# Eight unused words behind each 128-column block of the weights that TensorE loads

## The chip, the core and the metric

The kernel runs on one NeuronCore of one Trainium2 chip. The metric is the device time of one execution in microseconds (us), taken on the chip; lower is better. The profile is one execution that the hardware profiler recorded.

## The reference

Attention pools 12480 tokens of 128 channels into 32 rows (each of the 32 `inducing` rows attends to all tokens), every token then attends to the 32 pooled rows, and two feed-forward layers with 2048 hidden units follow, the first with a leaky rectifier, the second with `h * sigmoid(1.702 h)`.

```
def mab(q, kv):
    s = scale * (q @ kv.transpose(0, 2, 1))
    s = s - s.max(-1, keepdims=True)
    a = np.exp(s)
    a /= a.sum(-1, keepdims=True) + 1e-09
    return a @ kv
h = mab(I, x)            # I: the 32 inducing rows
x = mab(x, h)            # 12480 x 128
h = x @ w_in             # 128 -> 2048
x = np.maximum(0.01 * h, h) @ w_out        # 2048 -> 128
h = x @ w2_in
out = (h * (1.0 / (1.0 + np.exp(-1.702 * h)))) @ w2_out
```

The weights come as float64, x and `inducing` as float32.

## The kernel before

**Tiling.** The tokens are cut into 25 tiles. Tiles 0 and 24 have 352 tokens, the 23 between them 512. A tile lies channels by tokens, `[128, 512]`, so that a product has the tile as its moving operand and a block of 128 x 128 weights as its stationary operand. The 2048 hidden units are 16 blocks of 128 (`NF`).

**Precision.** Each float32 operand is split into two float32r halves (hi and lo), and a product is done as three passes: hi by hi, lo by hi, hi by lo. Weights are converted from float64 bits on the chip (`convert_stages`, the last step `upper` writes hi on ScalarE and lo on GpSimd) and then stay in SBUF.

**The layers.** `steps` runs over layer, tile and block, 800 steps in all. In a step `ffn_in` (L704) makes 128 hidden units of a tile in PSUM. In the first layer this is one product with `hw` (L709; the pooled rows are already multiplied into the first weights), in the second three products with the two halves of `w2` (L713 to L715). ScalarE and VectorE apply the activation and split it into `ghi` and `glo` (L723, L724 in the first layer, L729 to L731 in the second). `ffn_out` (L734) adds the block's part to the output tile `acc`, three products with the two halves of `v1` or `v2` (L741 to L743), `LOOK` = 3 steps behind. So a step is 4 products in the first layer and 6 in the second, 4000 in all, and each is preceded by the load of its own stationary block (LDWEIGHTS). The order is written out by hand (`manual_schedule`); the side work (conversion, attention weights of the next tiles, the linear part of the leaky unit) is hung on steps by the tables at the top.

**Where the weights lie.** `w1`, `w2` and `hw` are rows of 2048 words (4 bytes each) in every partition, a block being 128 neighbouring words, that is 512 bytes. `v1` and `v2` hold for each block hi and lo side by side, again 128 words each. So the byte addresses of all blocks of a matrix leave the same remainder by 512. In the built program that is 416 for every block of `hw`, `w1`, `w2`, `v1` and `v2`. The moving tiles `ghi`, `glo` and `at` begin at addresses that leave 480, `x2h` and `x2l` at addresses that leave 96. `w1` is a moving operand only (L638, where the stationary operands `hTl` and `hTh` leave 416 too); `w2` is put in the space of `w1` once that has been read.

Of the kernel before, what the change touches and what calls it, by code (L numbers as in the profile page):

```python
# [10 lines left out]
F32 = mybir.dt.float32  # L11
# [8 lines left out]
LOOK = 3  # blocks of hidden units between both products  # L20
TC = 4  # chunks of tokens in a token tile
ENDS = 88  # tokens of a chunk in the first and the last tile, 128 in the others
B = 32  # side of VectorE's transposed blocks
# [5 lines left out]
# pieces of x that blocks of weights are loaded before, the iterations of their conversion  # L29
W_LOADS = [6, 8]  # L30
W_STEPS = [0, 0, 1, 2, 2, 3]
# where the work beside the first two tiles goes, by their steps
# [14 lines left out]
def kernel(  # L47
# [10 lines left out]
    """float32 products run as float32r passes over halves: hi is a value's upper 12  # L58
    significant bits, lo = value - hi the others, both exact in float32r."""
# [23 lines left out]
    # token p * chunks + j of a part of x is row p of chunk j  # L83
# [4 lines left out]
    # token tiles that are loaded together  # L88
# [14 lines left out]
    def keep_busy(count):  # L103
        """TensorE's clock halves when it waits for long: products of zeros meanwhile."""
        for _ in range(count):
            nc.tensor.matmul(
                idle_ps[:, :256], idle[:, :P], idle[:, :256], start=True, stop=True
            )

# [1 line left out]
    CW = 512  # L111
    LOW = bits_f32(896 << 20)  # the words of 2^-127 and of float32's largest 2^127 * f
    HIGH = bits_f32((1150 << 20) | 0xFFEFF)

    def convert_stages(src, hi, lo):
        """src: [P, CW] of float64 bits. Its magnitude clamped to float32's range, sign,
        exponent and 23 fraction bits make a float32: hi is its rounding, lo the rest."""
        raw = conv.tile([P, 2 * CW], U32, tag="raw", name="raw", bufs=5)
        d = raw.rearrange("p (n w) -> p n w", w=2)
        v = conv.tile([P, CW], U32, tag="v", name="v", bufs=3)  # L120
        vf = v.bitcast(F32)
        if len(hi.shape) == 3:
            vo = vf.rearrange("p (f d) -> p f d", d=hi.shape[2])
        else:
            vo = vf

        def load():
            dst = raw if len(src.shape) == 2 else raw.rearrange(
                "p (f d) -> p f d", d=src.shape[2]
            )  # L130
            nc.sync.dma_start(out=dst, in_=src)

        def magnitude():
            nc.scalar.activation(out=vf, in_=d.bitcast(F32)[:, :, 1], func=AF.Abs)  # L134

        def clamp():
            nc.gpsimd.tensor_scalar(vf, vf, LOW, HIGH, op0=ALU.max, op1=ALU.min)  # L137

        def shift():
            nc.vector.tensor_scalar(  # L140
                v, v, 3, 0x3FFFFFFF, op0=ALU.logical_shift_left, op1=ALU.bitwise_and
            )

        def top():
            nc.vector.scalar_tensor_tensor(  # L145
                v, d[:, :, 1], 0xC0000000, v, op0=ALU.bitwise_and, op1=ALU.bitwise_or
            )

        def bottom():
            nc.vector.scalar_tensor_tensor(  # L150
                v, d[:, :, 0], 29, v, op0=ALU.logical_shift_right, op1=ALU.bitwise_or
            )

        def upper():
            nc.scalar.activation(out=hi, in_=vo, func=AF.Copy)
            nc.gpsimd.tensor_tensor(out=lo, in0=vo, in1=hi.bitcast(F32), op=ALU.subtract)  # L156

        return load, magnitude, clamp, shift, top, bottom, upper

    def matrix_in(src, name, tag):  # L160
        """[model, hidden]: a column block of hidden units is a stationary operand."""
        hi, lo = (wts.tile([P, DFF], F32R, name=f"{name}{h}", tag=f"{tag}{h}") for h in "hl")
        parts = []
        for o in range(0, DFF, CW):
            c = slice(o, o + CW)
            parts.append((src[:, c].bitcast(U32), hi[:, c], lo[:, c]))
        return (hi, lo), parts

    def matrix_out(src, name):
        """[hidden, model] by blocks of hidden units, hi and lo of a block side by side."""  # L170
        w = wts.tile([P, NF, 2, C], F32R, name=name)
        parts = []
        for o in range(0, DFF, CW):
            f = slice(o // P, (o + CW) // P)
            s = src[o : o + CW, :].bitcast(U32).rearrange("(f p) d -> p f d", p=P)
            parts.append((s, w[:, f, 0, :], w[:, f, 1, :]))
        return w, parts

    w1, w1_parts = matrix_in(moe_w_in, "w1", "w")
    v1, v1_parts = matrix_out(moe_w_out, "v1")  # L180

# [37 lines left out]
    # ---- pooling attention: a split of the softmax per quadrant of partitions, merged at  # L219
    # the end; each has a running maximum over the pieces ----  # L220
# [13 lines left out]
    nm = xnp.tile([P, NP], F32, name="nm")  # -SCALE * running maximum  # L234
# [29 lines left out]
    def scores(i):  # L264
        """Quadrant q: chunks q * n to q * n + n - 1 of the piece."""
        n = pieces[i]
        k = ch[starts[i]]
        w = n * k
        ps = s_t[i] = ps_h.tile([P, 512], F32, tag="h", name="s_ps")
        for q in range(NQ):  # L270
            b, o = divmod(q * n, TC)
            nc.tensor.matmul(  # L272
                ps[q * m : (q + 1) * m, :w], iT,
                xT[starts[i] + b][:, o * k : o * k + w], start=True, stop=True,
            )
        nc.vector.tensor_reduce(out=mx[:, i : i + 1], in_=ps[:, :w], axis=AX.X, op=ALU.max)
        if i == 0:
            nc.vector.tensor_scalar_mul(nm[:, :1], mx[:, :1], -SCALE)
        else:
            nc.vector.scalar_tensor_tensor(  # L280
                out=nm[:, i : i + 1], in0=mx[:, i : i + 1], scalar=-SCALE,
                in1=nm[:, i - 1 : i], op0=ALU.mult, op1=ALU.min,
            )
# [65 lines left out]
    def merge_max():  # L349
        """The quadrants' maxima, each beside the others of its row."""  # L350
# [129 lines left out]
    at_t = {}  # L480

    def weights_tile():
        """Rows (hi, lo, hi, lo) of a tile's weights, for rows (hi, hi, lo, lo) of what they
        weigh: all four products in one contraction."""
        return main.tile([P, TOK], F32R, tag="at", name="at", bufs=3)

    def token_tile(t):
        """One tile, tokens on partitions."""
# [59 lines left out]
    hl = [None] * NG  # by group: hi and lo of the weights, pooled row x token  # L548

    def token_group(g):  # L550
        """Four tiles, a tile's pooled rows on a quadrant of partitions."""
# [5 lines left out]
        def s0():  # L557
            ps = ps_h.tile([P, 512], F32, tag="h", name="s2_ps")
            for q, t in enumerate(tiles):
                # a short tile's own columns again behind it  # L560
# [56 lines left out]
    def rows_upper(dst, src, scale):  # L617
        """(hi, hi, lo, lo) by quadrants of scale * src, which is the same in each."""
# [10 lines left out]
    hTh, hTl = halves(hTf, "hT")  # L629
    hw = wts.tile([P, DFF], F32R, name="hw")  # L630
# [3 lines left out]
    def pooled_block(b):  # L634
        ps = hw_ps[b] = ps_h.tile([P, 512], F32, tag="h", name="hw_ps")
        c = slice(b * 512, (b + 1) * 512)
        for j, (a, w) in enumerate(((hTl, w1[1]), (hTl, w1[0]), (hTh, w1[1]), (hTh, w1[0]))):
            nc.tensor.matmul(ps, a, w[:, c], start=(j == 0), stop=(j == 3))  # L638

    def pooled_upper(b):  # L640
        rows_upper(hw[:, b * 512 : (b + 1) * 512], hw_ps[b], 1.0)

    def pooled_lower(b):
        rows_lower(hw[:, b * 512 : (b + 1) * 512], hw_ps.pop(b), 1.0)

    # the leaky unit is LEAK * h + (1 - LEAK) * relu(h); its linear part needs both
    # weights' product with the pooled rows alone
# [3 lines left out]
    def linear_transposed(b):  # L651
# [3 lines left out]
        for k in range(4):  # L655
            f = 4 * b + k
            nc.tensor.transpose(
                ps[:, k * P : (k + 1) * P], hw[:, f * P : (f + 1) * P].bitcast(F32), ident
# [5 lines left out]
    def linear_product(b):  # L664
        for k in range(4):
            f = 4 * b + k
            nc.tensor.matmul(
                lin_st["ps"][:, : 2 * C], lin_st[b][:, k, :],
                v1[:, f].rearrange("p h c -> p (h c)"),
# [7 lines left out]
    def linear_end():  # L677
        # hi and lo rows and columns added, the sum in each quadrant
# [8 lines left out]
    # pair[(s, k), (s', k')] = (k == k') for s in (0, 2)  # L687
# [16 lines left out]
    def ffn_in(l, t, f):  # L704
        ps = ps_h.tile([P, 512], F32, tag="h", name="h_ps")
        o = ps[:, : tok[t]]
        cols = slice(f * P, (f + 1) * P)
        if l == 0:
            nc.tensor.matmul(o, hw[:, cols], at_t[t], start=True, stop=True)  # L709
        else:  # L710
            hi, lo = x2h_t[t]
            wh, wl = late["w2"]
            nc.tensor.matmul(o, wh[:, cols], hi, start=True, stop=False)  # L713
            nc.tensor.matmul(o, wl[:, cols], hi, start=False, stop=False)  # L714
            nc.tensor.matmul(o, wh[:, cols], lo, start=False, stop=True)  # L715
# [31 lines left out]
    def x2_slot(t):  # L747
        """One that is free by then: its x and its group's weights have been read."""
# [18 lines left out]
    # work beside the layers, by the step that it goes with  # L767
# [5 lines left out]
    # the first weights' blocks as the first two tiles get to them  # L773
# [52 lines left out]
    late_matrix(matrix_in, moe2_w_in, "w2", ["w"], 60)  # L826
# [58 lines left out]
```

## Time and profile before

| | |
|---|---|
| time, median of 3 runs | 976.13 us (975.91 to 976.14) |
| profiled execution, span from its first to its last instruction | 974.8 us |
| median less that span: what lies around it | 1.3 us |
| TensorE products busy / weight loads busy | 963.9 us (99%) / 783.3 us (80%) |
| VectorE busy | 644.5 us (66%) |
| ScalarE busy | 787.8 us (81%) |
| GpSimd busy | 67.2 us (7%) |

The profiled execution's own time is known as its span; the median of the runs is 1.3 us longer. Products are pipelined: a product of 512 columns has a record of some 0.39 us, and the next begins 0.23 us after it began. So the busy share of TensorE tells only that a product was always under way. What the kernel pays for a product is the distance from its start to the next start, called its **pitch** below. It is read from the start times of a timeline, or as a stretch divided by the count of products in it.

### The profile page before, as it was taken

To read this page: it belongs to the slowest core of one execution; us is meant where nothing else is said; L and a number is where in the kernel's file an instruction comes from. 1 tells how busy PE (TensorE), PEld (TensorE's weight loads), DVE (VectorE), ACT (ScalarE), POOL (GpSimd) and SP (SyncE) were. 2 spreads that over 40 slices of the span, in tenths; PEclk is the share of its full clock that TensorE was granted. 3 is DMA by queue.
4 is the path that set the end of the run, shared out by engine and by line. 5 is a ranking of instruction groups with operands and counts; after the bars stand their busy time and mean duration, and the time that the engine had idled before them with its cause. 6 is when DMAs were issued, how large, how long until landed. Compare 5 with 4: busy or idle time off the path is not lost.

```text
span 974.8 us, 13366 instructions
## 1 busy us (share of the span) xinstructions
PE 963.9 (99%) x4630; PEld 783.3 (80%) x4630; DVE 644.5 (66%) x1049; ACT 787.8 (81%) x1378; POOL 67.2 (7%) x53
## 2 busy tenths in 40 slices
PE   9989999999999999999999999999999999999998
PEld 6667787887878878898888888888888888888887
DVE  4898788978878778765555555555555555555554
ACT  6576677767766666679999999999999999999997
POOL 1360021202200000000000000000000000000000
PEclk9999999999999999999999999999999999999999
DMA  9302120031000100000000000000000000000000
GB/s 340 98 1 55 33 65 22 7 93 33 23 23 7 27 12 23 8 1 8 12 11 12 11 12 22 11 11 11 12 12 12 11 11 18 16 12 12 12 11 19
DMA packets 15434, 27.99 MB, mean 29 GB/s; under 512 B 2358, under 2 KB 6870, under 8 KB 15366
## 3 DMA queue, kind: packets, MB, share of 16 engines
q1 hardware_dynamic: 15366, 27.14, 8.8%
q8 instruction: 36, 0.59, 0.2%
q14 instruction: 32, 0.26, 0.1%
HBM read 14.79 MB, written 6.39 MB: 22 GB/s over the span
## 4 chain that ended last, share of the span: by engine, by line
PE 96%; DVE 3%; DMA 0%; ACT 0%; issue 0%; SPq 0%; DVEq 0%; ACTq 0%
PE acc L743 18%; PE acc L742 18%; PE acc L741 18%; PE h_ps L715 9%; PE h_ps L713 9%; PE h_ps L714 9%; PE h_ps L709 9%; PE xT_ps L255 1%; DVE glo L724 1%; PE s_ps L272 1%; PE s_ps L563 1%; PE pv_ps L321 1%; PE acc L745 1%; PE p_ps L302 1%; DMA xn<-in_x_dram 0%; DVE v L145 0%
## 5 line engine op out<-in xcount | busy, mean ns | idle before, releaser
L731 DVE TENSOR_TENSOR glo<-g,ghi 128x512 fp32r<-128x512 f32 (+1 forms) x400 | 271.7, 679 | 238.9 <-ACT ghi L730 226.9
L723 ACT ACTIVATE ghi<-h_ps 128x512 fp32r<-128x512 f32 (+1 forms) x400 | 233.1, 587 | 101.6 <-PE h_ps L709 97.1
L743 PE MATMUL acc<-glo,v 128*128 128x512 f32 (+1 forms) x800 | 310.6, 388 | 0.8 <-DVE glo L724 0.6
L742 PE MATMUL acc<-ghi,v 128*128 128x512 f32 (+1 forms) x800 | 309.1, 386 | 0.5 <-POOL v L156 0.5
L741 PE MATMUL acc<-ghi,v 128*128 128x512 f32 (+1 forms) x800 | 308.2, 385 | 0.0
L724 DVE SCALAR_TENSOR_TENSOR glo<-h_ps,ghi 128x512 fp32r<-128x512 f32 (+1 forms) x400 | 263.4, 674 | 65.1 <-ACT ghi L723 61.7
L729 ACT ACTIVATE g<-h_ps 128x512 f32<-128x512 f32 (+1 forms) x400 | 234.8, 587 | 36.2 <-PE h_ps L715 0.5
L730 ACT ACTIVATE ghi<-g 128x512 fp32r<-128x512 f32 (+1 forms) x400 | 248.2, 620 | 12.6
L742 PEld LDWEIGHTS acc<-ghi,v 128*128 128x128 f32 x800 | 150.3, 188 | 33.5 <-POOL v L156 0.8
L743 PEld LDWEIGHTS acc<-glo,v 128*128 128x128 f32 x800 | 150.3, 188 | 33.2 <-DVE glo L724 3.5
L741 PEld LDWEIGHTS acc<-ghi,v 128*128 128x128 f32 x800 | 150.3, 188 | 28.6
L715 PE MATMUL h_ps<-x2l,w2h 128*128 128x512 f32 (+1 forms) x400 | 156.8, 392 | 0.0
L709 PE MATMUL h_ps<-at,hw 128*128 128x512 f32 (+1 forms) x400 | 155.4, 389 | 0.3 <-ACT at L543 0.3
L713 PE MATMUL h_ps<-x2h,w2h 128*128 128x512 f32 (+1 forms) x400 | 154.7, 387 | 0.0
L714 PE MATMUL h_ps<-x2h,w2l 128*128 128x512 f32 (+1 forms) x400 | 153.1, 383 | 0.0
L709 PEld LDWEIGHTS h_ps<-at,hw 128*128 128x128 f32 x400 | 75.1, 188 | 20.1 <-issue 3.6
L714 PEld LDWEIGHTS h_ps<-x2h,w2l 128*128 128x128 f32 x400 | 75.1, 188 | 16.1
L715 PEld LDWEIGHTS h_ps<-x2l,w2h 128*128 128x128 f32 x400 | 75.1, 188 | 15.6
L713 PEld LDWEIGHTS h_ps<-x2h,w2h 128*128 128x128 f32 x400 | 75.1, 188 | 15.5
L137 POOL TENSOR_SCALAR v<-v 128x512 f32<-128x512 f32 x16 | 31.7, 1983 | 59.3 <-ACT v L134 59.3
L759 ACT ACTIVATE x<-acc 128x512 f32<-128x512 f32 (+1 forms) x25 | 14.7, 587 | 7.7 <-PE acc L745 7.7
L762 DVE TENSOR_SCALAR o_t<-acc 128x512 f32<-128x512 f32 (+1 forms) x25 | 16.8, 671 | 0.5 <-PE acc L743 0.5
(117 smaller groups left out, 347.2 us busy)
## 6 DMA issues: line engine op xcount, KB each, us to landing
out_dram<-o_t SPq DMA_DIRECT2D x23, 256.0 KB, 2.0
xn<-in_x_dram SPq DMA_DIRECT2D x11, 512.0 KB, 9.8
raw<-in_moe_w_in_dram SPq DMA_DIRECT2D x8, 512.0 KB, 4.9
raw<-in_moe_w_out_dram SPq DMA_DIRECT2D x8, 512.0 KB, 4.2
at<-hlhi SPq DMA_DIRECT2D x44, 64.0 KB, 2.0
at<-hllo SPq DMA_DIRECT2D x44, 64.0 KB, 2.0
xn<-in_x_dram SPq DMA_DIRECT2D x2, 176.0 KB
out_dram<-o_t SPq DMA_DIRECT2D x2, 176.0 KB, 1.8
```

The lines of the kernel that those rows point to most:

```text
L709: nc.tensor.matmul(o, hw[:, cols], at_t[t], start=True, stop=True)
L713: nc.tensor.matmul(o, wh[:, cols], hi, start=True, stop=False)
L714: nc.tensor.matmul(o, wl[:, cols], hi, start=False, stop=False)
L715: nc.tensor.matmul(o, wh[:, cols], lo, start=False, stop=True)
L723: nc.scalar.activation(out=hi, in_=o, func=AF.Relu)
L724: nc.vector.scalar_tensor_tensor(out=lo, in0=o, scalar=0.0, in1=hi.bitcast(F32), op0=ALU.max, op1=ALU.subtract)
L729: nc.scalar.activation(out=g, in_=o, func=AF.Silu, scale=BETA)
L730: nc.scalar.activation(out=hi, in_=g, func=AF.Copy)
L731: nc.vector.tensor_tensor(out=lo, in0=g, in1=hi.bitcast(F32), op=ALU.subtract)
L741: nc.tensor.matmul(o, v[:, f, 0, :], hi, start=(f == 0), stop=False)
L742: nc.tensor.matmul(o, v[:, f, 1, :], hi, start=False, stop=False)
L743: nc.tensor.matmul(o, v[:, f, 0, :], lo, start=False, stop=end)
```

## The change

Every stationary block gets 8 unused words (32 bytes) behind it. A block of `hw` and `w2` then begins 544 bytes after the one before, and so do the hi and lo parts of `v1` and `v2`. Every place that reads or writes a whole run of blocks now names them as blocks by 128 columns instead of one run of 512 or 2048 columns. `w1` keeps its 512 bytes, by a skew of 0. The built program places the first block of each matrix at a remainder of 416 by 512 again, so block f of `hw` and `w2` leaves 416 + 32 f, less 512 where that is reached: 16 blocks, 16 remainders. The 32 parts of `v1` and of `v2` have each remainder twice. The moving tiles move by whole multiples of 512 bytes and leave 480 and 96 as before. The instructions stand in the same order on all five engines; of some of them the shape is written 128x4x128 instead of 128x512. (Comments, which the change takes out, are left out of the diff.)

```diff
+SKEW = 8
...
-    def matrix_in(src, name, tag):
-        hi, lo = (wts.tile([P, DFF], F32R, name=f"{name}{h}", tag=f"{tag}{h}") for h in "hl")
+    def matrix_in(src, name, tag, skew):
+        hi, lo = (
+            wts.tile([P, NF * (C + skew)], F32R, name=f"{name}{h}", tag=f"{tag}{h}")
+            .rearrange("p (f c) -> p f c", f=NF)[:, :, :C]
+            for h in "hl"
+        )
         parts = []
         for o in range(0, DFF, CW):
-            c = slice(o, o + CW)
-            parts.append((src[:, c].bitcast(U32), hi[:, c], lo[:, c]))
+            f = slice(o // C, (o + CW) // C)
+            parts.append((src[:, o : o + CW].bitcast(U32), hi[:, f], lo[:, f]))
...
-        w = wts.tile([P, NF, 2, C], F32R, name=name)
+        w = wts.tile([P, NF, 2, C + SKEW], F32R, name=name)[:, :, :, :C]
...
-    w1, w1_parts = matrix_in(moe_w_in, "w1", "w")
+    w1, w1_parts = matrix_in(moe_w_in, "w1", "w", 0)
...
-    hw = wts.tile([P, DFF], F32R, name="hw")
+    hw = wts.tile([P, NF, C + SKEW], F32R, name="hw")[:, :, :C]
...
-        rows_upper(hw[:, b * 512 : (b + 1) * 512], hw_ps[b], 1.0)
+        rows_upper(hw[:, 4 * b : 4 * b + 4], hw_ps[b].rearrange("p (f c) -> p f c", c=C), 1.0)
...
-        rows_lower(hw[:, b * 512 : (b + 1) * 512], hw_ps.pop(b), 1.0)
+        src = hw_ps.pop(b).rearrange("p (f c) -> p f c", c=C)
+        rows_lower(hw[:, 4 * b : 4 * b + 4], src, 1.0)
...
-                lin_st["ps"][:, : 2 * C], lin_st[b][:, k, :],
-                v1[:, f].rearrange("p h c -> p (h c)"),
+                lin_st["ps"][:, : 2 * C].rearrange("p (h c) -> p h c", h=2),
+                lin_st[b][:, k, :], v1[:, f],
...
-            nc.tensor.matmul(o, hw[:, cols], at_t[t], start=True, stop=True)
+            nc.tensor.matmul(o, hw[:, f], at_t[t], start=True, stop=True)
...
-            nc.tensor.matmul(o, wh[:, cols], hi, start=True, stop=False)
-            nc.tensor.matmul(o, wl[:, cols], hi, start=False, stop=False)
-            nc.tensor.matmul(o, wh[:, cols], lo, start=False, stop=True)
+            nc.tensor.matmul(o, wh[:, f], hi, start=True, stop=False)
+            nc.tensor.matmul(o, wl[:, f], hi, start=False, stop=False)
+            nc.tensor.matmul(o, wh[:, f], lo, start=False, stop=True)
...
-    late_matrix(matrix_in, moe2_w_in, "w2", ["w"], 60)
+    late_matrix(matrix_in, moe2_w_in, "w2", ["w", SKEW], 60)
```

## Rows read from the trace of the kernel before

**Rows 1.** The page: busy us, share of the span, instructions; TensorE's granted clock.

```profile
PE 963.9 (99%) x4630; PEld 783.3 (80%) x4630; DVE 644.5 (66%) x1049; ACT 787.8 (81%) x1378; POOL 67.2 (7%) x53
...
PEclk9999999999999999999999999999999999999999
```

**Rows 2.** The page: the chain that ended last, share of the span.

```profile
PE 96%; DVE 3%; DMA 0%; ACT 0%; issue 0%; SPq 0%; DVEq 0%; ACTq 0%
```

**Rows 3.** Windows, first and second layer: us, each engine's busy us, clock, DMA share, GB/s.

```profile
150.00:250.00 100.00, 100.00 (x443) 79.92 (x442) 83.28 (x133) 72.20 (x126) 17.79 (x13) 1.00 0.14 38
450.00:950.00 500.00, 500.00 (x2176) 408.38 (x2175) 278.57 (x409) 453.27 (x749) 0.00 (x0) 1.00 0.03 13
```

**Rows 4.** Timeline, TensorE, second layer: start us, us, instruction; first, last of 7.

```profile
700.81 0.39 PE L743 MATMUL acc<-glo,v 128*128 128x512 f32 x1
...
702.19 0.39 PE L743 MATMUL acc<-glo,v 128*128 128x512 f32 x1
```

**Rows 5.** Timeline, TensorE, first layer: first and last of 37 products.

```profile
302.45 0.39 PE L709 MATMUL h_ps<-at,hw 128*128 128x512 f32 x1
...
310.69 0.39 PE L709 MATMUL h_ps<-at,hw 128*128 128x512 f32 x1
```

**Rows 6.** Timeline, TensorE, second layer, first tile, 352 columns: first, last of 7.

```profile
440.60 0.32 PE L713 MATMUL h_ps<-x2h,w2h 128*128 128x352 f32 x1
...
441.56 0.32 PE L713 MATMUL h_ps<-x2h,w2h 128*128 128x352 f32 x1
```

**Rows 7.** Timeline, TensorE, start: idle bf16 products, merged (whole stretch, count); L638.

```profile
40.21 0.28 PE L106 MATMUL idle_ps<-idle 128*128 128x256 bf16 x1
...
45.23 1.36 PE L106 MATMUL idle_ps<-idle 128*128 128x256 bf16 x11
...
48.40 0.40 PE L638 MATMUL hw_ps<-w1h,hTl 128*128 128x512 f32 x1
48.63 0.39 PE L638 MATMUL hw_ps<-w1l,hTh 128*128 128x512 f32 x1
48.86 0.39 PE L638 MATMUL hw_ps<-w1h,hTh 128*128 128x512 f32 x1
49.09 0.49 PE L709 MATMUL h_ps<-at,hw 128*128 128x352 f32 x2
```

**Rows 8.** Groups by shape, TensorE, 450 to 950 us: count, busy us, mean ns, idle.

```profile
L715 PE MATMUL h_ps<-x2l,w2h 128*128 128x512 f32 x363 | 144.5, 398 | 0.0
L743 PE MATMUL acc<-glo,v 128*128 128x512 f32 x362 | 142.6, 394 | 0.0
L713 PE MATMUL h_ps<-x2h,w2h 128*128 128x512 f32 x363 | 142.4, 392 | 0.0
L742 PE MATMUL acc<-ghi,v 128*128 128x512 f32 x362 | 141.9, 392 | 0.0
L741 PE MATMUL acc<-ghi,v 128*128 128x512 f32 x362 | 141.2, 390 | 0.0
L714 PE MATMUL h_ps<-x2h,w2l 128*128 128x512 f32 x363 | 140.8, 388 | 0.0
```

**Rows 9.** Groups by shape, whole span: writers and readers whose shape changes.

```profile
L156 POOL TENSOR_TENSOR v<-v,v 128x512 fp32r<-128x512 f32 x8 | 10.7, 1331 | 45.6 <-ACT v L155 45.6
...
L156 POOL TENSOR_TENSOR w2l<-v,w2h 128x512 fp32r<-128x512 f32 x4 | 5.2, 1302 | 31.8 <-ACT w2h L155 31.8
L155 ACT ACTIVATE v<-v 128x512 fp32r<-128x512 f32 x8 | 5.0, 626 | 1.0 <-DVE v L150 1.0
L623 DVE SCALAR_TENSOR_TENSOR hw<-hw_ps,hw 64x512 fp32r<-64x512 f32 x4 | 2.8, 694 | 0.1
L667 PE MATMUL lin_ps<-v,hwT 128*128 128x256 f32 x16 | 2.5, 280 | 0.0
L155 ACT ACTIVATE w2h<-v 128x512 fp32r<-128x512 f32 x4 | 2.5, 624 | 0.0
...
L619 ACT ACTIVATE hw<-hw_ps 128x512 fp32r<-128x512 f32 x4 | 2.4, 599 | 1.8 <-PE hw_ps L638 1.8
```

More of the change, by code (lines that the diff above doesn't have):

```diff
@@ L635, in pooled_block @@
         ps = hw_ps[b] = ps_h.tile([P, 512], F32, tag="h", name="hw_ps")
-        c = slice(b * 512, (b + 1) * 512)
+        c = slice(4 * b, 4 * b + 4)
         for j, (a, w) in enumerate(((hTl, w1[1]), (hTl, w1[0]), (hTh, w1[1]), (hTh, w1[0]))):
-            nc.tensor.matmul(ps, a, w[:, c], start=(j == 0), stop=(j == 3))
+            nc.tensor.matmul(
+                ps, a, w[:, c].rearrange("p f c -> p (f c)"), start=(j == 0), stop=(j == 3)
+            )
     def pooled_upper(b):
-        rows_upper(hw[:, b * 512 : (b + 1) * 512], hw_ps[b], 1.0)
+        rows_upper(hw[:, 4 * b : 4 * b + 4], hw_ps[b].rearrange("p (f c) -> p f c", c=C), 1.0)
     def pooled_lower(b):
-        rows_lower(hw[:, b * 512 : (b + 1) * 512], hw_ps.pop(b), 1.0)
+        src = hw_ps.pop(b).rearrange("p (f c) -> p f c", c=C)
+        rows_lower(hw[:, 4 * b : 4 * b + 4], src, 1.0)
     lin = const.tile([P, C], F32R, name="lin")
@@ L657, in linear_transposed @@
             nc.tensor.transpose(
-                ps[:, k * P : (k + 1) * P], hw[:, f * P : (f + 1) * P].bitcast(F32), ident
+                ps[:, k * P : (k + 1) * P], hw[:, f].bitcast(F32), ident
             )
@@ L706, in ffn_in @@
         o = ps[:, : tok[t]]
-        cols = slice(f * P, (f + 1) * P)
         if l == 0:
-            nc.tensor.matmul(o, hw[:, cols], at_t[t], start=True, stop=True)
+            nc.tensor.matmul(o, hw[:, f], at_t[t], start=True, stop=True)
         else:
```

## The prediction

> **What bounds the kernel now.** The page first: TensorE has a product under way for 99% of the span, at a granted clock of 1.00 (the level of 2.4 GHz) in every slice [rows 1], and the chain that ended last runs on TensorE for 96% [rows 2]. A busy share of 99% tells little where records overlap, so the windows come next: in the second layer 500 us hold 2176 products, with the first and the last of them cut, so the pitch is 500/2175 = 0.2299 us; no other engine is full there, ScalarE being busy for 453 of the 500 us [rows 3]. The timeline gives the same: six products from 700.81 to 702.19, 0.230 us each [rows 4]. In the first layer 36 pitches take 8.24 us, 0.2289 each [rows 5]. A product of 352 columns has 0.96/6 = 0.160 us [rows 6].
>
> These pitches are nearly the whole time. The 23 tiles of 512 tokens make 368 steps in each layer: 368 x 4 x 0.2289 = 337 us and 368 x 6 x 0.2299 = 508 us. The two short tiles make 32 steps in each: 32 x 10 x 0.160 = 51 us. That is 896 of the 974.8 us; the other 79 us are the start, ahead of the layers, and the side work between the steps. So the kernel's time is 3680 long pitches and 320 short ones, and this change can only matter through the pitch.
>
> The pitch is longer than the columns ask for. 512 columns at 2.4 GHz are 0.213 us. The idle bf16 products at the start stream 256 columns each, with a load ahead of each one: 11 of them take 1.36 us, and less the last record (0.28 for a single one) that leaves 0.108 us a pitch [rows 7], or 0.216 for 512 columns. The float32r products lose some 0.013 us against that, in both layers. Whatever causes this is what the change could touch: while one product streams its tile out of SBUF, the next one's block is read from SBUF too.
>
> **The change, part by part.**
>
> *Instructions.* None is added or removed and none moves; the DMAs keep their sizes and their places in SP's queue, and no wait is added. The sum starts from zero.
>
> *Writers of the wider blocks.* ScalarE's and GpSimd's last conversion step of w2 now writes four pieces of 128 words with a gap. The conversion of v1 and v2 already does this: hi and lo of a block lie side by side, so each of its writes skips every second 128 words. It takes 626 ns on ScalarE and 1331 on GpSimd, against 624 and 1302 for w2h and w2l that are written in one run [rows 9]. So a gap costs 2 ns on ScalarE and up to 29 on GpSimd, and all of it lies under the products of the first layer, GpSimd having nothing to do in the second [rows 3]; without that cover it would be 4 x 31 ns = 0.1 us. The four writes of hw by ScalarE (599 ns) and VectorE (694 ns) [rows 9] may be waited for by the first products; by the same comparison they grow by some 2 ns each, 0.02 us in all. I take nothing for both.
>
> *The linear part's product, L667.* Its moving operand, hi and lo of a block of v1, is now two runs of 128 columns. There are 16 of them, 280 ns each [rows 9]. From below: nothing. From above: each is done like two products, 16 x 0.28 = 4.5 us more. I take nothing: the same words are streamed, with one jump in them, and the writers show what a jump costs, 2 to 29 ns for three of them [rows 9].
>
> *The loads.* 4000 loads, all from another remainder than before, or for one block in sixteen the same. The trace of before shows three distances between the remainder of the moving tile and that of the block which is loaded beside it. For ghi, glo and at it is 480 - 416 = 64, for x2h and x2l it is 96 - 416 + 512 = 192, and for w1 at L638, whose blocks and stationary operands all leave 416, it is 0. The pitches: 0.2289 us in the first layer, all at 64 [rows 5]; 0.69/3 = 0.230 at 0 [rows 7]; 0.2299 for the second layer, half at 64 and half at 192 [rows 4]. By line, the records at 192 (L713 to L715) are 392, 388 and 398 ns, mean 392.7, those at 64 (L741 to L743) 390, 392 and 394, mean 392.0 [rows 8]. Three distances, one of them the same remainder on both sides, and a mean that moves by 1 ns at most. There is a reason why it should move little: a load goes through all 512 bytes of its block and a product through 2048 bytes of its tile, so each passes every remainder whatever it starts from. A shift changes when they meet, not whether. Against that stands that single lines of the same distance differ by 10 ns, steadily over 363 products [rows 8]: something in the meeting does depend on the start.
>
> So the step's value lies between two ends. Below: every long product goes at the pace of the quickest line, L714, 388 against a mean of 392.3: 3680 x 4.3 ns = -16 us. Above: every one goes at that of L715, 398: 3680 x 5.7 = +21 us. With 16 remainders the blocks take a mean over many meetings, and the mean over those that the trace has is what the kernel pays now. I take nothing.
>
> The Trainium skill speaks against the change ("SBUF — State Buffer", section "Who interferes with whom"): TensorE reads the moving operand and the weight load through two independent ports, and waits for nobody. By that rule the addresses can't matter, and the sum is 0; the mean pitches at three distances agree with it, the 10 ns between lines do not obviously. Another page prices the pitch of 512 columns at 215.7 ns ("TensorE: Matmul & The Clock Gate", "Wait — 56ns, not 53.3ns?"); the trace has 229 to 230, so some 14 ns of each pitch are not in it, an estimate of 3680 x 14 ns = 52 us that the first rule doesn't explain either.
>
> The sum is 0 us to within what a measurement of this kernel can tell, which I put at 0.2%, 2 us. The profiled execution is 974.8 us long and the median of the runs 976.13, 1.3 us around the span; 976 us is forecast.
>
> **The rivals.**
>
> *Faster.* Load and stream do get in each other's way at certain remainders, and equal remainders for every block keep the collisions in step: the same line has the same record 363 times over, which speaks for it. Spread remainders would break that. For it also stands the 13 ns over the bf16 pitch; all of it would be 3680 x 13 = 48 us, and of each short one 160 - 352/256 x 108 = 11 ns, 4 us more: 924 us. Against it stands that distances of 0, 64 and 192 cost the same. If it goes this way I expect the pace of the quickest line for half the products or all of them: 968 to 960 us. No other engine would stop it: ScalarE needs 453/500 of the second layer's time now [rows 3], and a pitch 4 ns shorter asks 2% more.
>
> *Slower.* Some remainders collide more than the one that all blocks share now, and 416 happens to be a good one. The place is each long product of the second layer, where one line in six is already at 398 ns. It decides from a mean pitch that is 0.53 ns longer (2 us over 3680). Half the blocks at L715's pace would be +10 us, 986 us; a quarter of them +5 us, 981 us. For it: the first layer, all at a distance of 64, is 1 ns quicker than the second, so a mixture may cost the first layer up to 1 ns, 1472 x 1 ns = 1.5 us. Against it: the mean at 192 is within 1 ns of that at 64.
>
> *A reader by pieces is slower.* L667 at the upper end above, +4.5 us, 980.6 us, if it were all on TensorE's path; 3% of chance, counted with slower.
>
> That the change doesn't do what it says can be left out: the built program has the 16 remainders.
>
> **How the numbers follow.** No change has 0.46: three distances with one pitch, and a sum with nothing else in it. Faster has 0.31, since 13 ns of each pitch are unexplained and a steady pattern by line is what a collision would look like. Slower has 0.23, by the same sensitivity to the start and the 1 ns between the layers, with the piecewise reader in it. For the range, the faster cases reach 960 us; leaving out those near the full gain (0.1) gives 962. Of the slower ones those up to a quarter of the blocks are kept: 981, with 0.08 above. The likeliest case's own range is 974.2 to 978.1.
>
> **What would show it.** If right: the windows of both layers hold the same counts as [rows 3] to within three products in 500 us, the first layer's 36 pitches take 8.2 to 8.3 us, and the lines' records, though no longer the same for all blocks, keep a mean of 392 ns. Records of L741 to L743 that now differ by block f at the same line would show that remainders count; equal ones would show that they don't, and that the pattern by line has another cause. L619, L623 and L155 should stay within 5 ns, L667 within 10. The prediction is wrong if the mean record of 512 columns moves by more than 0.5 ns; below 391.8 is the first rival, above 392.8 the second.

## The result, and the profile after

The changed kernel takes 984.04 us (median of 4 runs, 982.85 to 986.64) against 976.13; the ratio is 1.0076, with a 95% interval of 1.0055 to 1.0097. It is slower by 8 us, and 3 us over the top of the range. The profiled execution's span is 982.1 us, 7.3 more than before.

The page of the changed kernel: TensorE has a product under way as long as before, to the per cent, and the chain is on it as before.

```profile
PE 971.3 (99%) x4630; PEld 784.1 (80%) x4630; DVE 645.3 (66%) x1049; ACT 788.5 (80%) x1378; POOL 66.8 (7%) x53
...
PE 96%; DVE 3%; ACT 0%; DMA 0%; issue 0%; SPq 0%; ACTq 0%; DVEq 0%
```

The same windows as [rows 3], of the changed kernel, and one at the start:

```profile
40.00:60.00 20.00, 17.29 (x105) 13.74 (x106) 17.08 (x42) 12.04 (x26) 8.58 (x6) 0.91 0.08 27
150.00:250.00 100.00, 100.00 (x437) 78.90 (x436) 82.07 (x130) 70.93 (x123) 17.55 (x12) 1.00 0.14 38
450.00:950.00 500.00, 500.00 (x2172) 406.90 (x2171) 277.70 (x409) 451.62 (x749) 0.00 (x0) 1.00 0.03 13
```

The first layer has 437 products in 100 us where it had 443, the second 2172 in 500 us where it had 2176 (19 of the 2172 are short ones of the tile before). So each layer is slower by itself, the first by 1.4%, the second by less, and no new wait shows in the chain. At 40 to 60 us the granted clock was 0.91 in this execution and 1.00 in the profiled one of the kernel before. Among the runs of both kernels are some at a mean clock of 1.000 and some at 0.998; the one run of the changed kernel at 1.000 had a span of 981.1, so some 1 us of the 7.3 may be that, an estimate from a single run.

Now the products by line, 150 to 250 us (first layer) and 450 to 950 us (second layer): count, busy us, mean ns of a record, idle. In the changed file the lines of the first layer are L716 and L748 to L750, those of the second L720 to L722 and L748 to L750.

```profile
L716 PE MATMUL h_ps<-at,hw 128*128 128x512 f32 x104 | 41.2, 396 | 0.0
L748 PE MATMUL acc<-ghi,v 128*128 128x512 f32 x104 | 41.1, 395 | 0.0
L750 PE MATMUL acc<-glo,v 128*128 128x512 f32 x103 | 40.7, 395 | 0.0
L749 PE MATMUL acc<-ghi,v 128*128 128x512 f32 x103 | 40.6, 394 | 0.0
```

```profile
L721 PE MATMUL h_ps<-x2h,w2l 128*128 128x512 f32 x361 | 142.2, 394 | 0.0
L722 PE MATMUL h_ps<-x2l,w2h 128*128 128x512 f32 x360 | 141.4, 393 | 0.0
L720 PE MATMUL h_ps<-x2h,w2h 128*128 128x512 f32 x361 | 141.1, 391 | 0.0
L749 PE MATMUL acc<-ghi,v 128*128 128x512 f32 x357 | 140.6, 394 | 0.0
L748 PE MATMUL acc<-ghi,v 128*128 128x512 f32 x357 | 140.4, 393 | 0.0
L750 PE MATMUL acc<-glo,v 128*128 128x512 f32 x357 | 140.4, 393 | 0.0
```

The same window of the first layer before:

```profile
L709 PE MATMUL h_ps<-at,hw 128*128 128x512 f32 x106 | 41.7, 393 | 0.0
L743 PE MATMUL acc<-glo,v 128*128 128x512 f32 x105 | 41.2, 393 | 0.0
L742 PE MATMUL acc<-ghi,v 128*128 128x512 f32 x105 | 41.1, 391 | 0.0
L741 PE MATMUL acc<-ghi,v 128*128 128x512 f32 x105 | 41.1, 391 | 0.0
```

Its mean was 392 ns; now it is 395, which is 3.0 ns on each of 1472 products, 4.4 us. In the second layer the steady pattern of 388 to 398 ns by line [rows 8] is gone: all lines have 391 to 394 ns, as averages over 16 blocks that now differ, and the mean has gone from 392.3 to 393.0. The stretch from 460 to 920 us holds long products alone. Before and after, it reads:

```profile
460.00:920.00 460.00, 460.00 (x2001) 375.71 (x2000) 255.44 (x375) 416.63 (x688) 0.00 (x0) 1.00 0.03 13
460.00:920.00 460.00, 460.00 (x1993) 373.86 (x1992) 254.51 (x374) 415.22 (x685) 0.00 (x0) 1.00 0.03 12
```

With the count less one, the pitch went from 460/2000 = 0.2300 us to 460/1992 = 0.2309, 0.9 ns on 2208 products, 2.0 us. A record is longer than its pitch by the same 162 ns in both kernels (392.3 against 230.0, 393.0 against 230.9), so that a difference between records can be read as one between pitches.

The conversion's writes are unmoved (w2h 624 ns on ScalarE, w2l 1302 on GpSimd, hw 598 and 694 on ScalarE and VectorE), and the linear part's product in two runs has its 280 ns as in [rows 9].

### The profile page after: what moved, and what is told of

It is laid out like the page before. It is cut to its first block, busy times and chain, and to the rows that moved or that the text cites. A ratio compares the mean times of both kernels' runs of the same rounds, so it can differ in the third digit from the quotient of the medians.

```text
span 982.1 us, 13366 instructions
## 1 busy us (share of the span) xinstructions
PE 971.3 (99%) x4630; PEld 784.1 (80%) x4630; DVE 645.3 (66%) x1049; ACT 788.5 (80%) x1378; POOL 66.8 (7%) x53
## 4 chain that ended last, share of the span: by engine, by line
PE 96%; DVE 3%; ACT 0%; DMA 0%; issue 0%; SPq 0%; ACTq 0%; DVEq 0%
PE acc L750 18%; PE acc L748 18%; PE acc L749 18%; PE h_ps L721 9%; PE h_ps L722 9%; PE h_ps L720 9%; PE h_ps L716 9%; PE xT_ps L260 1%; DVE glo L731 1%; PE s_ps L277 1%; PE s_ps L568 1%; PE pv_ps L326 1%; PE acc L752 1%; PE p_ps L307 0%; DMA xn<-in_x_dram 0%; DVE hw L628 0%
## 5 line engine op out<-in xcount | busy, mean ns | idle before, releaser
L750 PE MATMUL acc<-glo,v 128*128 128x512 f32 (+1 forms) x800 | 311.7, 390 | 0.7 <-DVE glo L731 0.6
L748 PE MATMUL acc<-ghi,v 128*128 128x512 f32 (+1 forms) x800 | 311.3, 389 | 0.0
L750 PEld LDWEIGHTS acc<-glo,v 128*128 128x128 f32 x800 | 150.6, 188 | 35.0 <-DVE glo L731 2.4
L748 PEld LDWEIGHTS acc<-ghi,v 128*128 128x128 f32 x800 | 150.4, 188 | 32.5
L716 PE MATMUL h_ps<-at,hw 128*128 128x512 f32 (+1 forms) x400 | 156.9, 393 | 0.3 <-ACT at L548 0.2
L721 PE MATMUL h_ps<-x2h,w2l 128*128 128x512 f32 (+1 forms) x400 | 155.3, 388 | 0.0
L722 PE MATMUL h_ps<-x2l,w2h 128*128 128x512 f32 (+1 forms) x400 | 154.9, 387 | 0.0
L720 PE MATMUL h_ps<-x2h,w2h 128*128 128x512 f32 (+1 forms) x400 | 154.1, 385 | 0.0
L716 PEld LDWEIGHTS h_ps<-at,hw 128*128 128x128 f32 x400 | 75.5, 189 | 21.1 <-issue 4.4
L720 PEld LDWEIGHTS h_ps<-x2h,w2h 128*128 128x128 f32 x400 | 75.1, 188 | 16.1
L722 PEld LDWEIGHTS h_ps<-x2l,w2h 128*128 128x128 f32 x400 | 75.1, 188 | 15.2
```

The costliest lines, as they stand in the source:

```text
L716: nc.tensor.matmul(o, hw[:, f], at_t[t], start=True, stop=True)
L720: nc.tensor.matmul(o, wh[:, f], hi, start=True, stop=False)
L721: nc.tensor.matmul(o, wl[:, f], hi, start=False, stop=False)
L722: nc.tensor.matmul(o, wh[:, f], lo, start=False, stop=True)
L748: nc.tensor.matmul(o, v[:, f, 0, :], hi, start=(f == 0), stop=False)
L750: nc.tensor.matmul(o, v[:, f, 0, :], lo, start=False, stop=end)
```

## The experiments

The times in this section stand against runs of the kernel before on the same chip; intervals are of 95%.

**Is it the code in blocks, or the remainders, and in which layer?** Four kernels, from the changed one.

With no unused words, but the block-wise code (four numbers, one for each matrix, stand in the places of `SKEW`):

```diff
-SKEW = 8
+SKEW_HW, SKEW_V1, SKEW_W2, SKEW_V2 = 0, 0, 0, 0
```

> The changed kernel with 0 unused words: all its block-wise reads and writes stay, the blocks stand 512 bytes apart again and all leave 416. If the cut into blocks or the new shapes cost the 8 us (theory of form), 984 us. If the remainders do, by sequence or by distance, 976 us, and second-layer records of 388 to 398 ns by line as before.

976.62 us, ratio 0.9993 (0.9981 to 1.0006): the form costs nothing, or 0.6 us at most by the interval. The second layer's lines have 388, 390, 392, 392, 394 and 398 ns again.

The words in the first layer's weights alone (the numbers below; 0, 0, 8, 8 in the run after it):

```diff
-SKEW = 8
+SKEW_HW, SKEW_V1, SKEW_W2, SKEW_V2 = 8, 8, 0, 0
```

> Unused words in the first layer's weights alone (hw, v1); w2 and v2 stand 512 bytes apart. Theory of remainders: the first layer's pitch goes from 0.229 to 0.2324 us, 1472 products of 512 columns x 3.3 ns = 5 us, so 981 us, while the second layer keeps its mean record of 392.3 ns. Theory of form: the layers share the 8 us by their products, 3 us here, 979.

981.44 us, ratio 1.0048 (1.0033 to 1.0063), 4.7 us by the ratio.

> Unused words in the second layer's weights alone (w2, v2). Theory of remainders: 2208 products x 0.9 ns = 2 us, so 978 us, with the first layer at 0.229 us a product again. Theory of form: 5 us here, 981.

979.23 us, ratio 1.0021 (1.0011 to 1.0031), 2.1 us. Each layer has the loss that the theory of remainders gave it (5 and 2 us), and together, 6.8 us, they are the whole to within the intervals (7.4 us by the ratio of the changed kernel). The layer without the words has its records of before in both runs, to within 1 ns.

16 unused words, so that all blocks stay at 32 by 64:

```diff
-SKEW = 8
+SKEW_HW, SKEW_V1, SKEW_W2, SKEW_V2 = 16, 16, 16, 16
```

> 16 unused words (64 bytes) behind each block instead of 8: only 8 remainders, all of them 32 by 64 as before, where the change alternates between 0 and 32 by 64. If any change of the remainder between neighbouring loads disturbs the pitch (theory of the sequence), 984 us within 2. If blocks that begin at the other half of 64 bytes are what costs, half of the loss or all of it goes: 976 to 980 us.

987.27 us, ratio 1.0108 (1.0092 to 1.0123). Slower yet, so it is not the cause that blocks begin at the other half of 64 bytes. Neither form of the expectation had foreseen a larger loss. It lies in the second layer above all: its pitch is 460/1974 = 0.2330 us, 3.0 ns more than before, while the first layer's mean record is some 394 ns, 2.4 more.

**Is it the change of remainder from block to block, or the distance from the moving tile to the block?** No unused words, all blocks at one remainder, but all weights moved together by a pad ahead of them, and a second pad behind them that keeps the moving tiles where they were (8 words; 16, 32 and 64 in the next three):

```diff
+    pads = [wts.tile([P, n], F32, name=f"pad{n}") for n in (8,)]
+    pads.append(conv.tile([P, 120], F32, name="rest", bufs=1))
     w1, w1_parts = matrix_in(moe_w_in, "w1", "w", 0)
```

> No unused words behind the blocks, but all weights together 32 bytes higher, the moving tiles where they were: every block leaves 448, the distances from tile to loaded block are 32 (first layer and half of the second) and 160. Theory of distance (each product's pitch follows from the remainder of its tile less that of the block that is loaded beside it): the changed kernel's first layer had 234.3 ns at 32, so the first layer grows by 5.3 ns x 1472 = 8 us, 984 us. Theory of sequence (only a change of remainder from one block to the next disturbs): 229 ns and 976 us.

992.57 us, ratio 1.0164 (1.0149 to 1.0179). 32 bytes in the place of all weights, and nothing else, cost 16 us. With equal remainders throughout there is no sequence to disturb: the place of the weights does it, by itself or against that of the tiles. The theory of the sequence falls. Windows of this run:

```profile
150.00:250.00 100.00, 100.00 (x436) 78.50 (x435) 81.91 (x130) 70.77 (x124) 17.55 (x12) 1.00 0.14 38
460.00:920.00 460.00, 460.00 (x1963) 369.75 (x1963) 251.27 (x368) 409.20 (x676) 0.00 (x0) 1.00 0.03 12
```

The loss is twice the 8 us, which counted the first layer alone: the second, at 32 and 160, has a pitch of 460/1962 = 0.2345 us, 4.5 ns more on 2208 products, 10 us. The first layer pays less than was expected: its mean record is 396 ns, some 4 ns more and not 5.3.

> All weights 64 bytes higher: every block leaves 480, as the moving tiles ghi, glo and at do; distances 0 and 128. The run with 64 unused bytes had its slowest mean pitch at distance 0, 237 ns. Theory of distance: first layer 232 to 237 ns, 980 to 988 us. Theory of sequence: 229 ns, 976 us.

978.81 us, ratio 1.0025 (1.0013 to 1.0036). The time is neither of the two expected. The layers go apart: the first, at distance 0, has records of 391, 390, 390 and 389 ns, less than before and far from the 237 ns of pitch (a record of 399) that single products at distance 0 had in the run with 64 bytes; the second, at 0 and 128, has a pitch of 460/1982 = 0.2321 us. There the three products at distance 0 are the longer ones, with 393 to 397 ns against 391 to 393 for those at 128.

> All weights 128 bytes higher: every block leaves 32; distances 448 and 64. Theory of distance: the changed kernel had 231.7 ns at 448, so 231.7 - 229 = 2.7 ns x 1472 = 4 us, 980 us. Theory of sequence: 976 us.

982.09 us, ratio 1.0078 (1.0052 to 1.0104). The second layer of this run, by line:

```profile
L724 PE MATMUL h_ps<-x2l,w2h 128*128 128x512 f32 x362 | 142.6, 394 | 0.0
L752 PE MATMUL acc<-glo,v 128*128 128x512 f32 x358 | 142.5, 398 | 0.0
L723 PE MATMUL h_ps<-x2h,w2l 128*128 128x512 f32 x362 | 141.9, 392 | 0.0
L722 PE MATMUL h_ps<-x2h,w2h 128*128 128x512 f32 x362 | 141.2, 390 | 0.0
L750 PE MATMUL acc<-ghi,v 128*128 128x512 f32 x359 | 140.9, 392 | 0.0
L751 PE MATMUL acc<-ghi,v 128*128 128x512 f32 x358 | 138.9, 388 | 0.0
```

This is [rows 8] with the two halves of the step exchanged: x2h, x2h and x2l have the 390, 392 and 394 that ghi, ghi and glo had, and these have the 392, 388 and 398. Before, ghi and glo were at 64 and x2 at 192; here x2 is at 64 and ghi and glo at 448. So 448 acts as 192: distances count by 256, and the steady pattern by line belongs to the distance, not to the line.

> All weights 256 bytes higher: every block leaves 160; distances 320 and 448. Theory of distance: 230.9 ns at 320 in the changed kernel, 2 ns x 1472 = 3 us, 979 us, and half of the second layer as at 448. Theory of sequence: 976 us.

976.22 us, ratio 0.9997 (0.9986 to 1.0007): a move by 256 bytes changes nothing, and each line's record is that of [rows 8] to the ns. The expectation, which took distances by 512, missed the first layer by 2 ns for that reason.

**A block's own place, or the distance?** Weights and moving tiles moved together (the first pad of u_448 without the second):

> No unused words; the weights and the moving tiles all 32 bytes higher: blocks leave 448, ghi, glo and at leave 0, x2h and x2l leave 128. The distances 64 and 192 are those of before. Theory of distance: 976 us, the second layer's records by line as before (388 to 398 ns). Theory of the place (a block's own remainder decides, 448 being a bad one): 992 us, as when the weights alone stood at 448.

976.94 us, ratio 1.0007 (0.9996 to 1.0018). With the blocks at the same 448 that cost 16 us, nothing is lost as long as the tiles are moved too: it is the distance, and not the block's own place. Three of the six lines of the second layer:

```profile
L723 PE MATMUL h_ps<-x2l,w2h 128*128 128x512 f32 x363 | 144.5, 398 | 0.0
...
L749 PE MATMUL acc<-ghi,v 128*128 128x512 f32 x362 | 141.2, 390 | 0.0
L722 PE MATMUL h_ps<-x2h,w2l 128*128 128x512 f32 x363 | 140.9, 388 | 0.0
```

**Every product at one distance.** x2h and x2l (and with them `g`, the linear part's sums and the output tile, which lie behind the same pad) are moved to the remainder of the other moving tiles by a pad of 96 words, and the weights to 480 less the distance (for distance 0 pads of 16 and 112 words, as above):

```diff
+        main.tile([P, 96], F32, name="rest2", bufs=1)
         s = lin_st["s"] = main.tile([P, 2, C], F32, tag="lins", name="lins", bufs=1)
```

> No unused words; weights at 480, and x2h and x2l moved to 480 as well, so that every product has distance 0. Theory of distance: both layers at the 227.2 ns that the first layer had at distance 0, so 1472 x 1.9 ns + 2208 x 2.8 ns = 9 us less than before, 967 us. If the order of the operands decides rather than the distance: the second layer stays at 230 to 232 ns, 974 to 979 us.

967.19 us, ratio 0.9907 (0.9891 to 0.9922): faster than both kernels, at the time that the distance gave. Windows of this run, as [rows 3]:

```profile
150.00:250.00 100.00, 99.93 (x446) 80.42 (x445) 83.75 (x134) 72.57 (x127) 18.52 (x13) 1.00 0.14 38
450.00:950.00 500.00, 500.00 (x2214) 414.76 (x2213) 282.06 (x415) 459.08 (x761) 0.00 (x0) 1.00 0.04 13
```

> Every product at distance 128 (weights at 352, all moving tiles at 480). Theory of distance with a period of 256 bytes: the changed kernel's products at 128 and 384 had 232.6 ns, so 3.6 ns x 1472 + 2.6 ns x 2208 = 11 us, 987 us, if a product's distance alone counts; if the products before it count too, a pitch of its own between 226 and 236 ns in both layers alike, 960 to 1000 us.

987.88 us, ratio 1.0119 (1.0103 to 1.0135), within 1 us of what the distance gave.

> Every product at distance 224 (weights at 256, all moving tiles at 480). As at 128: the changed kernel's products at 224 and 480 had 231.6 ns, so 2.6 ns x 1472 + 1.6 ns x 2208 = 7 us, 983 us, if the product's own distance alone counts; otherwise one pitch in both layers between 226 and 236 ns.

990.40 us, ratio 1.0146 (1.0130 to 1.0162). This is 7 us over the 983 that single products at this distance in the changed kernel gave.

> Every product at distance 96 (weights at 384, moving tiles at 480). The changed kernel's products at 96 and 352 had some 234 ns: 5 ns x 1472 + 4 ns x 2208 = 16 us, 992 us. If the changed kernel's loss is the mean over the distances, the pitches at 96 and 160 have a mean of some 232 ns: the other six are 227, 233, 229, 233, 233 and 233, and the changed kernel's mean over both layers is 231.5.

990.33 us, ratio 1.0148 (1.0127 to 1.0170), against 992 expected. The second layer of this run, three of its six lines; the others have the same three records:

```profile
L723 PE MATMUL h_ps<-x2h,w2h 128*128 128x512 f32 x357 | 142.4, 399 | 0.0
...
L725 PE MATMUL h_ps<-x2l,w2h 128*128 128x512 f32 x357 | 140.7, 394 | 0.0
L724 PE MATMUL h_ps<-x2h,w2l 128*128 128x512 f32 x357 | 140.0, 392 | 0.0
```

All products are at one distance here, and yet one in three is 5 to 7 ns longer than the others.

> Every product at distance 160 (weights at 320, moving tiles at 480). The changed kernel's products at 160 and 416 had some 232 ns: 3 ns x 1472 + 2 ns x 2208 = 9 us, 985 us. For the mean over the distances as in the run at 96.

993.24 us, ratio 1.0174 (1.0155 to 1.0192), the slowest place tried, 8 us over the 985 expected.

For distance 16 the weights begin 4 words into their tiles:

> Every product at distance 16 (weights at 464, moving tiles at 480). If the chip tells addresses apart in units of 32 bytes or more: 227 ns and 967 us as at distance 0, or 233 ns and 990 us as the first layer had at distance 32. If it goes on in smaller units: a pitch of its own, between the two, 230 ns and some 977 us.

971.47 us, ratio 0.9950 (0.9934 to 0.9967). The distance counts in steps under 32 bytes; 16 lies nearer to 0 than to 32, and not half way as expected.

**The block that is loaded beside a product, or the product's own?** As the kernel with distance 0, with 8 words ahead of hw alone:

```diff
+    pads.append(wts.tile([P, 8], F32, name="pad_a"))
     hw = wts.tile([P, NF, C + SKEW_HW], F32R, name="hw")[:, :, :C]
+    pads.append(wts.tile([P, 120], F32, name="pad_b"))
```

> As the run with every product at distance 0, but hw alone 32 bytes higher, so that a product beside which a block of hw is loaded (the one with glo in the first layer) has distance 224. If the block loaded beside a product counts: the record of the glo product in the first layer changes most, by up to 6 ns, one product in four, so 1472 x 1.5 ns = 2 us over the 967 us, 969 us. If the block that the product itself uses counts: the same time, but the product of hw with at has the changed record. The second layer stays as at distance 0.

972.86 us, ratio 0.9962 (0.9948 to 0.9976): 5.7 us over the kernel at distance 0, not 2. The first layer of this run:

```profile
L721 PE MATMUL h_ps<-at,hw 128*128 128x512 f32 x105 | 41.4, 394 | 0.0
L755 PE MATMUL acc<-glo,v 128*128 128x512 f32 x104 | 41.2, 396 | 0.0
L753 PE MATMUL acc<-ghi,v 128*128 128x512 f32 x104 | 40.9, 394 | 0.0
L754 PE MATMUL acc<-ghi,v 128*128 128x512 f32 x104 | 40.8, 392 | 0.0
```

The same window with distance 0 throughout, the run all_0:

```profile
L719 PE MATMUL h_ps<-at,hw 128*128 128x512 f32 x106 | 41.5, 391 | 0.0
L753 PE MATMUL acc<-glo,v 128*128 128x512 f32 x106 | 41.4, 390 | 0.1
L751 PE MATMUL acc<-ghi,v 128*128 128x512 f32 x106 | 41.3, 389 | 0.0
L752 PE MATMUL acc<-ghi,v 128*128 128x512 f32 x106 | 41.3, 389 | 0.0
```

The glo product, beside which hw is loaded, changed most, by 6 ns; but the other three changed too, by 3 to 5 ns, though their distances did not. So the records speak for the block that is loaded beside a product, as expected, and the disturbance goes on into the next products. That one product's distance alone fixes its own pitch is not so; the unequal lines of all_96 say the same.

**The distances together.** The mean record of the first layer is over its four lines in 150 to 250 us; the pitch of the second layer is 460 us by the count between 460 and 920 us less one.

| distance by 256 | first layer, mean record, ns | second layer, pitch, us | run |
|---|---|---|---|
| 0 | 390 | 460/2030 = 0.2266 | all_0 |
| 16 | 391 | 460/2015 = 0.2283 | all_16 |
| 32 | 396 | (0.2345 with half of it at 160) | u_448 |
| 64 | 392 | (0.2300 with half of it at 192) | before |
| 96 | 396 | 460/1972 = 0.2333 | all_96 |
| 128 | 395 | 460/1980 = 0.2323 | all_128 |
| 160 | 397 | 460/1964 = 0.2342 | all_160 |
| 192 | 395 | (0.2299 with half of it at 64) | u_32 |
| 224 | 396 | 460/1972 = 0.2333 | all_224 |

## Why the prediction was wrong

**What held.** The bound: the time is the pitch of 4000 products, and it moved with nothing else on the page changed. The terms at nothing: e1_zero shows that code in blocks costs nothing, the writers kept their records to within 3 ns and L667 its 280 ns, and no wait appeared. The second rival was the case: the words in it, that some remainders collide more than the one that all blocks share now and that 416 is a good one, are what the runs show, and its price of 5 to 10 us holds the 8 us. Its place was wrong for the larger part: it set the loss in the second layer and up to 1.5 us in the first, but the first pays 4.7 us and the second 2.1. That its price fits is partly luck. The prediction's own sign for it, a mean record above 392.8 ns, is there: 393.0 in the second layer and 395 in the first.

**The step that failed** is the value of the loads: "With 16 remainders the blocks take a mean over many meetings, and the mean over those that the trace has is what the kernel pays now. I take nothing." The second half is wrong. The kernel before had distance 64 in all of the first layer and half of the second, and among the multiples of 32 that is the cheapest but one: 392 ns in the first layer, where 0 has 390 and the other six have 395 to 397. Sixteen remainders replaced it by a mixture at 395 ns, 3.0 ns on 1472 products; the second layer's pitch grew by 0.9 ns on 2208. The term put at nothing is 4.7 us in the first layer and 2.1 in the second.

The first half, that a mixture costs the mean, fits the first layer: the eight distances of the table have a mean of 394.6 ns, so (394.6 - 392) x 1472 = 4 us. It is no rule. The run with 64 unused bytes has the distances 0, 64, 128 and 192 alone; in the first layer their mean in the table is 393 ns, and the run has some 394. In the second, the pitches of 0 and 128 and twice the 0.2300 us of 64 and 192 in turns have a mean of 0.2297 us; the run has 0.2330. So a mixture can cost more than the mean of its distances, and the fit in the changed kernel's first layer may be chance.

**Why the rows misled.** The prediction drew on three distances, 0, 64 and 192, "and a mean that moves by 1 ns at most". At 0 it had three pitches of the start, 0.230 us, read from stamps of 0.01 us; a difference of 3 ns can't be read there, and the steady pitch at 0 is 0.2266. The trace of before has another such stretch, at the first products of L638, and it gives 0.68/3 = 0.227:

```profile
43.74 0.39 PE L638 MATMUL hw_ps<-w1h,hTl 128*128 128x512 f32 x1
43.97 0.39 PE L638 MATMUL hw_ps<-w1l,hTh 128*128 128x512 f32 x1
44.20 0.39 PE L638 MATMUL hw_ps<-w1h,hTh 128*128 128x512 f32 x1
44.42 0.97 PE L497 MATMUL s_ps<-hT,xT 128*128 128x32 f32 x8
```

The two stretches together would have shown how little either can carry. At 64 and 192 it had the two halves of one step of the second layer, whose means agree at 392.0 and 392.7. But products do not stand alone, as hw_apart shows: the second layer at 64 and 192 in turns has 0.230 in before and in u_32, while a first layer all at 192 has 395 ns, against 392 at 64. What looked like two distances at one price was one pattern of the two together. And the argument that a load passes every remainder wherever it starts, so that a shift "changes when they meet, not whether" and should move little, is refuted by u_448: the same blocks, the same tiles, 32 bytes closer, 16 us.

**The warning that was in the rows** is the one that the prediction itself set against its value: lines of one distance differing by 10 ns over 363 products. It gave that sensitivity to both signs, and put the largest chance on the middle. What it did not draw is that a kernel at one remainder sits on one point of an unknown curve. The change then costs nothing only if that point is a middling one, and for the distances 32, 96, 128, 160 and 224 no row told.

**The rule of two ports.** The Trainium skill's "SBUF — State Buffer", section "Who interferes with whom", has TensorE read both operands through independent ports and wait for nobody. The runs differ: addresses alone move the whole kernel from 0.9907 to 1.0174 of its time. The measurement decides. In the steady layers the blocks of weights are read by TensorE's loads alone, so a load costs more or less by its address. That its partner is the stream of the moving tile is argued from u_32, where the two halves of the step exchange their records as their tiles exchange distances, and from both_32up; by which circuit, no run here tells.

**The first rival** was half right too: of the 13 ns over the bf16 pitch, 2 to 3 go with the distance and are got back at distance 0, but not by spreading the remainders. What makes up the other 10 ns stays open: distance 0 still has 0.2266 us against the 0.216 estimated from the idle bf16 products.

**What stays open.** How the disturbance passes from a product to the next, and so why single products at one distance have other pitches in a mixture (in the run with 64 unused bytes, 237 ns at distance 0) than in a kernel all at that distance. So what a mixture of distances costs can't be worked out from the table. No run moves x2h and x2l without `g`, on which ScalarE and VectorE work. Distances between 0 and 32 other than 16, and just below 256, were not tried, so a better place than 0 is not excluded.

## What to carry to other kernels

Where TensorE's pitch is the time, the byte distance by 256 between the moving tile and the block that is loaded beside it is a setting worth 2.7% between the best and the worst place tried (967 and 993 us), and 0.9% against the layout that the kernel had, for no instruction: pad so that all moving tiles share one remainder and all stationary blocks the same one, and measure a few distances. Don't spread the remainders in the hope of a gain: both spreads tried here lost, 8 us with 32 bytes and 10 us with 64, and a tuned kernel may sit on a good distance by luck; equally, any new small tile ahead of the weights or of the moving tiles moves that point unnoticed. And three pitches from a rounded timeline can't carry an argument about 3 ns: count products over a long window.

## What the runs showed of the hardware

- With float32r operands of 128 x 128 (load) and 128 x 512 (stream), the steady pitch goes from 0.2266 us at distance 0 to 0.2342 at 160 by 256, at a granted clock of 1.00 in both layers.
- The effect repeats after 256 bytes (u_160 against before: ratio 0.9997), depends on the difference and not on either place (both_32up, a common move by 32 bytes: 1.0007), and is there at 16 bytes (0.2283 us).
- At 64 and 192 in turns by three, six products settle into a pattern with mean records of 388 to 398 ns by line over 363 steps, and it goes with the distance when the weights are moved by 128 bytes.
- One product's distance does not fix its own pitch: all at 96, the lines have 399, 392 and 394 ns in turn; with hw alone moved by 32 bytes, the three products of a step whose distance stayed have 3 to 5 ns more.
